# Attention with a seven-product query projection, exponentials summed by pairs of key blocks, and a new split of the PSUM banks

## Chip, cores and metric

The kernel runs on one core of one Trainium2 chip. The metric is the device time of one execution in microseconds (us). Several executions are timed and medians are quoted. All runs in this document were fast (granted TensorE clock 0.998 to 1.0 over the whole execution). Profiled figures come from one execution of each kernel.

Engines are named as the profile names them. PE is TensorE (matrix products), PEld is its weight loads, DVE is VectorE, ACT is ScalarE, and SP issues the DMA transfers. In these traces each of them takes its instructions in the order in which the program gives them. PSUM is the memory into which PE writes its products; it is used here in banks of 512 fp32 columns. An eviction is the copy of a bank out of PSUM by DVE.

## The reference

The reference is one transformer block with modulation. Only its first half, attention, is changed. Cut to that:

```python
# x: [1, 2048, 1024], k_cache and v_cache: [1, 32, 2048, 128], wq: [1024, 4096], wo: [4096, 1024], all bf16
h = _layernorm(x) * (1 + ca) + sa
q = (h @ wq).reshape(B, Sq, 32, 128).transpose(0, 2, 1, 3)
scores = jnp.einsum('bhqd,bhkd->bhqk', q, k_cache) * 128 ** -0.5
p = _softmax(scores, axis=-1)
o = jnp.einsum('bhqk,bhkd->bhqd', p, v_cache)
x = x + ga * (o.transpose(0, 2, 1, 3).reshape(B, Sq, 4096) @ wo)
# ... then a gated MLP with a spatial product, untouched by the change
```

## The kernel before

The unit to think in is a **half**: one head with 1024 of the 2048 queries, over 16 key blocks of 128 keys. There are 64 halves, indexed by `i`; `kb` is the key block in a half. For each key block PE computes a block of scores (keys on partitions, two matmuls of 512 queries), ACT takes the exponential of the 128x1024 block, and PE multiplies it with the values (two more matmuls). DVE adds the 16 blocks of exponentials into one block `pacc`, which gives the softmax denominators. Between these, PE does the query projection of a coming half: 16 matmuls, from the list `fill`, a few in each key block.

So a half has 32 score matmuls, 32 value matmuls and 16 projection matmuls, 80 in all, each 128x128 weights with 512 columns.

The query projection, eight matmuls (the 1024 channels in steps of 128) into one PSUM bank for 512 queries, and then one copy out by DVE:

```python
def side_ps(name, shape):
    return psum.tile(shape, FP32, name=name, tag="side", bufs=1)   # 1 PSUM bank
# bank_ps: 3 banks (value products and others); wide_ps: 2 tiles of 2 banks (scores)

def q_work(h, qh, new_ps=side_ps, outs=None):
    ...
        def one(n, j=j, box=box):
            ...
            nc.tensor.matmul(box["ps"][:], wq_t[:, dc, hc:hc + DH], src[:, dc, q0:q0 + 512],
                             start=(n == 0), stop=(n == KD - 1))
            if n == KD - 1 and outs is None:
                out(j, box)                        # DVE: copy the bank to qT
```

The loop over key blocks (cut):

```python
for g, (i, kb) in enumerate(steps):
    if kb == 0:
        o_ps = [bank_ps("ops", [P, 512]) for _ in range(2)]
    ...
    if i == len(halves) - 1:
        ...
        elif kb == 13:
            normalise(i - 1)                       # DVE: ou * rbc; rbc comes by DMA
    pt = att.tile([P, 1024], BF16, name="pt", tag="pt", bufs=5)
    nc.scalar.activation(pt[:], s_tiles.pop(g)[:], ACT.Exp, scale=SCALE)
    emit_s(g + 2)                                  # scores, two key blocks ahead
    ...
    for j in range(2):                             # value products of this key block
        nc.tensor.matmul(o_ps[j][:], vs[h][:, kb, :], pt[:, j * 512:(j + 1) * 512],
                         start=(kb == 0), stop=(kb == NKB - 1))
    if kb == 1:
        nc.vector.tensor_add(out=pacc[:], in0=pt_tiles[g - 1][:], in1=pt[:])
    elif kb > 1:
        nc.vector.tensor_add(out=pacc[:], in0=pacc[:], in1=pt[:])   # 15 dependent additions a half
    ...                                            # at kb 15 DVE copies o_ps to ou, one bank
    ...                                            # before this addition, one after it
    for fn in fill[:n]:                            # projection matmuls of a coming half
        fn()
```

The output projection and all later large products already use seven products of half size instead of eight (class `Block`). The query projection did not.

The softmax here doesn't subtract the row's maximum and nothing guards it: scores larger than these inputs give would overflow.

## Time and profile before

| | |
|---|---|
| median before | 1782.42 us (4 runs, 1782.16 to 1783.58) |
| profiled execution: span | 1780.5 us |
| start of the first exponential | 30.63 us |
| first exponential to the end of the last | 1119.92 us |
| from there to the end | 629.91 us |
| a half in the steady stretch | 17.29 us, for 80 matmuls |

The length of a half is read as the distance between the starts of DVE's first output copy (`ou<-ops`) in successive halves.

The head of the page of the kernel before gives the span, the busy time of each engine, and, in its part on the chain of work that ended last, the share of each engine in that chain:

```profile
span 1780.5 us, 25079 instructions
PE 1751.8 (98%) x8526; PEld 809.6 (45%) x8644; DVE 1490.5 (84%) x2567; ACT 1296.6 (73%) x1527; POOL 27.6 (2%) x39
...
PE 90%; DVE 6%; issue 2%; DMA 2%; ACT 0%; SPq 0%; POOL 0%; DVEq 0%; ACTq 0%; POOLq 0%
```

(`issue` is time in which an engine waited for nothing that the profile shows; names with a q are sequencers.) PE is both the busiest engine and 90% of the chain. The busy share alone would not settle it: 98% in this kernel. The Trainium skill, "Perfetto Trace Analysis", section "Identifying the Most-Contended Engine", calls matmul busy time no good measure of how close a kernel is to the roofline, because pipelined instructions look smaller in a trace. Here the chain and the timeline were read instead.

The timeline of PE in the steady stretch (start in us, duration, engine, source line, operation, output and inputs, partitions x elements, number of instructions in the row):

```profile
702.01 0.59 PE L379 MATMUL sps<-qT,kT 128*128 128x512 bf16 x2
702.44 0.59 PE L648 MATMUL ops<-pt,v_sb 128*128 128x512 bf16 x2
702.87 0.38 PE L358 MATMUL qps<-h1T,wq_t 128*128 128x512 bf16 x1
703.09 0.59 PE L379 MATMUL sps<-qT,kT 128*128 128x512 bf16 x2
```

Five matmuls start in 703.09 - 702.01 = 1.08 us, 0.216 us each, without a break (over long stretches 0.2159). The durations overlap, as the matmuls are pipelined, so it is the distance of starts that counts. 80 x 0.2159 = 17.27 us, within 0.02 us of a half. Here a matmul that is left out is worth 0.216 us, as long as nothing else sets the pace.

What the rest is shows in DVE's own timeline:

```profile
701.69 0.69 DVE L662 COPY ou<-ops 128x512 f32<-128x512 f32 x1
702.29 0.68 DVE L657 TENSOR_TENSOR pacc<-pt 128x1024 bf16<-128x1024 bf16 x1
...
708.21 3.87 DVE L659 TENSOR_TENSOR pacc<-pacc,pt 128x1024 bf16<-128x1024 bf16 x5
```

The copy and the addition after it have nothing to do with each other: they start 0.60 us apart although each lasts 0.68 to 0.69 (they overlap by 0.09). In the last row each addition needs the sum of the one before: five take 3.87 us, so they start (3.87 - 0.69) / 4 = 0.79 us apart.

Busy time in a window of 200 us of the steady stretch (columns as in the header), and all that PE waited for between the first and the last exponential (engine and line of the waiting instruction, what it waited for: us in total, number of waits, longest; waits of 0.15 us or less are not listed):

```profile
core 0: us, PE busy (x) PEld busy (x) DVE busy (x) ACT busy (x) POOL busy (x), PEclk, DMA share, GB/s
600.00:800.00 200.00, 199.05 (x909) 90.44 (x926) 175.40 (x279) 183.66 (x185) 0.00 (x0) 1.00 0.49 126
```

```profile
PE ops L648 <- DVE ou L655: 1.1, 3, 0.6
PE dps L482 <- DVE qT L348: 0.9, 2, 0.7
PE sps L379 <- ACT pt L636: 0.9, 2, 0.7
PE qps L358 <- DVE rec L486: 0.4, 1, 0.4
```

DVE is 175.40 / 200 = 87.7% busy and ACT 91.8%. PE waits 3.3 us in 1119.

### The profile page before, as it was taken

How to read it: one execution, taken by the hardware profiler on the slowest of the kernel's cores; microseconds unless marked ns; L12 is line 12 of the kernel's file. 1: busy time of each engine (PE TensorE's matmuls, PEld its weight loads, DVE VectorE, ACT ScalarE, POOL GpSimd, SP SyncE). 2: the span in 40 equal slices, each digit the busy share in tenths (PEclk: the TensorE clock that was granted, in tenths of full speed). 3: DMA queues.
4: the chain of work that ended last, by engine and by line, in shares of the span. 5: the costliest groups of instructions: out<-in, count | busy, mean ns of one | idle time of the engine just before them, and what ended most of it. 6: DMA issues, size and time to landing. Idle time of an engine off the chain costs nothing.

```text
span 1780.5 us, 25079 instructions
## 1 busy us (share of the span) xinstructions
PE 1751.8 (98%) x8526; PEld 809.6 (45%) x8644; DVE 1490.5 (84%) x2567; ACT 1296.6 (73%) x1527; POOL 27.6 (2%) x39
## 2 busy tenths in 40 slices
PE   7999999999999999999999999999999999999999
PEld 4444444444444444444444444444444444444444
DVE  6998888888888888888889888896679789775894
ACT  6898999999989999999999999811145666733610
POOL 1000000000000000000000000000000000000000
PEclk9999999999999999999999999999999999999999
DMA  8584656566455535455555633635658374564312
GB/s 248 128 178 99 148 149 142 136 155 158 109 140 151 137 96 151 118 135 159 132 160 138 153 102 95 175 106 174 162 153 226 90 172 123 177 148 136 89 48 71
DMA packets 445345, 247.84 MB, mean 139 GB/s; under 512 B 289312, under 2 KB 406560, under 8 KB 445216
## 3 DMA queue, kind: packets, MB, share of 16 engines
q1 hardware_dynamic: 445216, 246.23, 52.7%
q8 instruction: 67, 1.10, 0.3%
q14 instruction: 62, 0.51, 0.1%
HBM read 144.18 MB, written 52.71 MB: 111 GB/s over the span
## 4 chain that ended last, share of the span: by engine, by line
PE 90%; DVE 6%; issue 2%; DMA 2%; ACT 0%; SPq 0%; POOL 0%; DVEq 0%; ACTq 0%; POOLq 0%
PE ops L648 23%; PE sps L379 23%; PE a L762 15%; PE qps L358 12%; PE b L762 8%; PE c L762 4%; PE bo L1363 3%; DVE pacc L659 1%; DVE sum L810 1%; DMA wm<-in_w_mod_dram 1%; DMA oq<-oT_dram 1%; PE mps L185 0%; DVE stats L138 0%; PE a L1441 0%; DVE z_st L1098 0%
## 5 line engine op out<-in xcount | busy, mean ns | idle before, releaser
L636 ACT ACTIVATE pt<-sps 128x1024 bf16<-128x1024 f32 x1024 | 1018.7, 1024 | 105.2 <-PE sps L379 71.3
L659 DVE TENSOR_TENSOR pacc<-pacc,pt 128x1024 bf16<-128x1024 bf16 x882 | 605.5, 687 | 59.1 <-ACT pt L636 1.6
L648 PE MATMUL ops<-pt,v_sb 128*128 128x512 bf16 x1992 | 597.4, 379 | 6.6 <-DVE ou L655 1.1
L379 PE MATMUL sps<-qT,kT 128*128 128x512 bf16 x2000 | 598.5, 379 | 1.5 <-ACT pt L636 0.9
L358 PE MATMUL qps<-h1T,wq_t 128*128 128x512 bf16 x990 | 334.9, 379 | 1.4 <-DVE rec L486 0.4
L648 PEld LDWEIGHTS <-v_sb 128*128 128x128 bf16 x2048 | 200.1, 98 | 243.1 <-issue 1.5
L379 PEld LDWEIGHTS <-kT 128*128 128x128 bf16 x2048 | 198.9, 98 | 243.9 <-issue 6.6
L805 ACT ACTIVATE snap<-a 128x512 f32<-128x512 f32 (+1 forms) x114 | 62.7, 566 | 126.4 <-PE a L762 113.9
L358 PEld LDWEIGHTS <-wq_t 128*128 128x128 bf16 x992 | 97.0, 98 | 117.1
L1212 ACT ACTIVATE zr<-zr,z_nm,z_rs 128x256 f16<-128x256 f16 x166 | 83.0, 592 | 77.6 <-DMA zr<-z_dram 70.9
L348 DVE CAST qT<-qps 128x512 bf16<-128x512 f32 x124 | 85.7, 691 | 40.2 <-PE qps L358 39.3
L810 DVE TENSOR_TENSOR sum<-b,snap 128x512 f32<-128x512 f32 (+1 forms) x76 | 50.3, 662 | 48.6 <-PE b L762 28.7
L762 PEld LDWEIGHTS <-h_slots 128*128 128x128 f16 (+1 forms) x574 | 56.2, 98 | 66.2 <-issue 0.9
L495 DVE TENSOR_TENSOR oT<-ou,rbc 128x1024 bf16<-128x1024 f32 x62 | 75.6, 1219 | 2.3 <-DMA rbc<-rec_dram 2.0
L762 PEld LDWEIGHTS <-zr 128*128 128x128 f16 x456 | 44.6, 98 | 54.1 <-issue 0.4
L473 DVE TENSOR_REDUCE den<-pT 128x8 f32<-128x1024 bf16 x54 | 63.9, 1183 | 0.0
L762 PEld LDWEIGHTS <-oq 128*128 128x128 bf16 (+1 forms) x408 | 39.7, 98 | 49.3 <-DMA oq<-oT_dram 1.4
L655 DVE COPY ou<-ops 128x512 f32<-128x512 f32 x63 | 43.6, 691 | 21.2 <-PE ops L648 21.2
L1066 ACT ACTIVATE z<-sum 128x448 f16<-128x448 f32 x48 | 27.6, 575 | 26.0 <-DVE sum L810 25.7
L657 DVE TENSOR_TENSOR pacc<-pt 128x1024 bf16<-128x1024 bf16 x63 | 43.0, 683 | 2.4 <-ACT pt L636 2.4
L1363 PE MATMUL bo<-w_out,z1T 128*128 128x512 f16 x192 | 44.2, 379 | 0.0
L662 DVE COPY ou<-ops 128x512 f32<-128x512 f32 x63 | 43.2, 685 | 0.0
(305 smaller groups left out, 1609.0 us busy)
## 6 DMA issues: line engine op xcount, KB each, us to landing
rbc<-rec_dram SPq DMA_DIRECT2D x63, 512.0 KB
v_sb<-in_A_v_cache_dram SPq DMA_DIRECT2D x40, 512.0 KB
oT_dram<-oT SPq DMA_DIRECT2D x62, 256.0 KB
sums_dram<-pacc SPq DMA_DIRECT2D x54, 256.0 KB
wm<-in_w_mod_dram SPq DMA_DIRECT2D x12, 1024.0 KB
zr<-z_dram SPq DMA_DIRECT2D x23, 512.0 KB
wo<-in_A_wo_dram SPq DMA_DIRECT2D x16, 512.0 KB
oq<-oT_dram SPq DMA_DIRECT2D x15, 512.0 KB
```

The costliest lines, as they stand in the source:

```text
L348: nc.vector.tensor_copy(out=out_t[:, sl], in_=box["ps"][:])
L358: nc.tensor.matmul(box["ps"][:], wq_t[:, dc, hc:hc + DH], src[:, dc, q0:q0 + 512], start=(n == 0), stop=(n == KD - 1))
L379: nc.tensor.matmul(sps[:, j * 512:(j + 1) * 512], kts[h][:, kb * P:(kb + 1) * P], qts[(h, qh)][:, j * 512:(j + 1) * 512], start=True, stop ...
L473: nc.vector.tensor_reduce(out=den[:], in_=state[i]["pT"][:], op=ALU.add, axis=mybir.AxisListType.X)
L495: nc.vector.tensor_mul(out=oT, in0=state[i]["ou"][:], in1=state[i]["rbc"][:])
L636: nc.scalar.activation(pt[:], s_tiles.pop(g)[:], ACT.Exp, scale=SCALE)
L648: nc.tensor.matmul(o_ps[j][:], vs[h][:, kb, :], pt[:, j * 512:(j + 1) * 512], start=(kb == 0), stop=(kb == NKB - 1))
L659: nc.vector.tensor_add(out=pacc[:], in0=pacc[:], in1=pt[:])
L762: nc.tensor.matmul(self.ps[self.BANK[n]], a, b, start=(n in (1, 2, 7) and k == 0), stop=(k == len(lhs) - 1), skip_group_check=True)
L810: nc.vector.tensor_add(out=t, in0=ps, in1=snap)
L1212: nc.scalar.activation(z, z, ACT.Identity, scale=z_rs[:, q:q + 1], bias=z_nm[:, q:q + 1])
L1363: nc.tensor.matmul(bo, z1T[0, f // 2][:, f % 2, ti * P:(ti + 1) * P], wout[f // 2][:, f % 2, sl], start=(f == 0), stop=(f == NF - 1), skip ...
```

## The change

The intent is to take matmuls off PE, which paces attention, and to pay for them on DVE.

1. **Seven products instead of eight.** For the head pairs 5 to 14 (heads 10 to 29) the query projection of two heads and all 2048 queries is cut into 2 x 2 x 2 blocks and computed with seven half-size products on sums of blocks: 56 matmuls instead of 64 for a pair, 80 fewer in all. DVE makes the operand sums (fp16) and combines the products, with 14 evictions of PSUM banks for a pair instead of 8.
2. **Sums of exponentials by pairs of key blocks**: 7 additions of 2048 elements and one of 1024 for a half, instead of 15 of 1024.
3. **PSUM.** Three banks and one become two for value products and two (`qa`, `qb`) for the projection. The value products of key blocks 0 to 7 come one key block later, and two sets are issued at key block 8, so that DVE can empty both output banks before they are written again.
4. **Order.** A table `FILLS` says for each half how many projection matmuls go into each key block; tiles in SBUF are packed to make room; some weight loads move.

The diff, cut to its core:

```diff
-        return psum.tile(shape, dtype, name=name, tag="bank", bufs=3)
-    def side_ps(name, shape):
-        return psum.tile(shape, FP32, name=name, tag="side", bufs=1)
+        return psum.tile(shape, dtype, name=name, tag="bank", bufs=2)
+    def qa_ps(name, shape):
+        return psum.tile(shape, FP32, name=name, tag="qa", bufs=1)
+    def qb_ps(name, shape):
+        return psum.tile(shape, FP32, name=name, tag="qb", bufs=1)
...
+    def q_pair(n, j):
+        ...
+        def done(m):
+            a, b = box["a"][:], box["b"][:] if "b" in box else None
+            if m in (1, 6, 5):
+                nc.vector.tensor_copy(out=x if m == 6 else su, in_=a)
+            if m == 2:
+                out(h, 0, b, su)
+            elif m == 5:
+                out(h + 1, 1, b, su)
+            elif m == 3:
+                out(h + 1, 0, a, None)
+            elif m == 4:
+                out(h, 1, b, x)
+        def one(m, dc):
+            ...
+            nc.tensor.matmul(box["b" if m in (2, 7, 4) else "a"][:], *operand(m, dc),
+                             start=(m in (1, 2, 7) and dc == 0), stop=(dc == 3),
+                             skip_group_check=True)
+            if dc == 3:
+                done(m)
+        return [... for m in (1, 2, 6, 7, 5, 3, 4) for dc in range(4)]
...
-    FILL = [2, 1, 1, 1, 1, 1, 0, 1, 2, 1, 2, 2, 0, 0, 0, 1]
+    PAIRS = range(5, 15)
+    FILLS = {...
+             16: [3, 1, 1, 1, 1, 0, 1, 1, 0, 1, 1, 0, 1, 0, 1, 1],   # even halves 16..54
+             17: [3, 1, 1, 1, 0, 1, 1, 1, 0, 1, 1, 0, 1, 1, 0, 1],   # odd halves 17..55
+             56: [3, 1, 0, 1, 0, 1, 1, 0, 0, 1, 0, 1, 0, 1, 0, 0],
+             ...}
...
+        if 1 <= kb <= 8:
+            emit_pv(g - 1)
+        if kb >= 8:
+            emit_pv(g)
...
-        if kb == 1:
-            nc.vector.tensor_add(out=pacc[:], in0=pt_tiles[g - 1][:], in1=pt[:])
-        elif kb > 1:
-            nc.vector.tensor_add(out=pacc[:], in0=pacc[:], in1=pt[:])
+        if kb == 3:
+            sums2 = att.tile([P, 2, 1024], BF16, name="sums2", tag="sums2", bufs=1)
+            nc.vector.tensor_add(out=sums2[:], in0=pairs[g // 2 - 1][:], in1=pairs[g // 2][:])
+        elif kb % 2 and kb > 3:
+            nc.vector.tensor_add(out=sums2[:], in0=sums2[:], in1=pairs[g // 2][:])
         if kb == NKB - 1:
+            pacc = state[i]["pacc"] = ...
+            nc.vector.tensor_add(out=pacc[:], in0=sums2[:, 0], in1=sums2[:, 1])
```

The products 1, 6, 5 and 3 of a group accumulate in one bank, `qa`, one on top of the other, and DVE must copy out each partial sum before the next product goes on top of it.

## The prediction

> **What bounds the kernel now.** TensorE: the page gives PE 98% busy and 90% of the chain that ended last. Attention runs from the first exponential at 30.6 us to the last at 1149.5 us. The timeline at 700 us shows 512-column matmuls 0.216 us apart without a break; a half (16 key blocks of one head, 1024 queries) takes 17.28 us = 80 x 0.216: 32 scores, 32 value products, 16 query projections. My estimate for the part is 5100 x 0.216 = 1102 us plus about 14 us for small products, 1116 in all, so only about 4 us are lost, nearly all before 168 us. The waits view has PE waiting for DVE or ACT under 4 us in all. DVE is 86 to 90% busy here, ACT 91%; exponentials last 1024 ns but follow each other in 0.924 us where PE lets them (5 in 4.72 us), so ACT alone would need about 946 us.
>
> **What the change does.**
> 1. For heads 10 to 29 the query projection of two heads becomes seven half-sized products instead of eight: 56 matmuls instead of 64 per pair. The instruction order confirms 80 fewer. Worth 80 x 0.216 = 17.3 us, all on the critical engine.
> 2. DVE gains work: 14 evictions per pair instead of 8 (60 more, 0.69 us each), 40 weight differences of 512 elements (about 0.4 us, estimated), 16 activation sums of 1024 (0.69 us): 41 + 16 + 11 = 68 us.
> 3. To pay, exponentials are summed by pairs of key blocks: per half seven additions of 2048 (1.22 us, as the trace has for that shape) and one of 1024, 9.2 us, instead of fifteen of 0.687, 10.3 us: 70 us less. The Trainium skill, "VectorE: DVE Perf Modes", tier table, gives bf16 tensor_tensor 2x; 683 and 1218 ns for 1024 and 2048 elements agree: doubling saves only the fixed part. DVE's total stays, but a half shrinks to 78 matmuls, 16.85 us, so I expect DVE 90 to 93% busy.
> 4. PSUM goes from three banks plus one to two plus two. Value products start one step late in each half, so that DVE can empty both output banks: about 1.5 us of other matmuls cover two copies that start 0.61 us apart. The tight place in a seven-product group is from product 5 to 3 in one bank; the fill table leaves a step there.
> 5. Late loads and banks are rearranged; I expect 1 to 2 us either way.
>
> **Sum.** 17.3 us gained, less 3 to 4 us of new PE waits on DVE (evictions behind 1.22 us additions): about 1768 us. Range 1763 to 1778. Chances: faster by over 2% 0.02, within 2% 0.95, slower by over 2% 0.03.
>
> **What would show each step.** The last exponential starts near 1135 us; from 250 to 900 us a half takes about 16.9 us; 80 matmuls fewer at the same 0.216 us; 448 additions of 2048 elements at about 1.22 us; PE waits for DVE grow from about 3 to 5 to 8 us; ACT stays below 95% busy; from the last exponential to the end stays 631 us within 2 us.
>
> **What would make it wrong.** If DVE's in-order queue sets the pace (over 96% busy, PE waiting for query evictions in most groups), the gain shrinks to a few us or vanishes. If the packed early tiles wait for one another, the first exponential comes later than 30.6 us. If later output-weight loads or the slot order stall the output projection, the loss appears right after the last exponential. If the delayed value products remove stalls that I do not see, the gain exceeds 17 us.

## More of the kernel before

The costliest groups on the page (line, engine, operation, shapes, count | busy us, mean ns of one | idle time of the engine just before them, and what ended most of it):

```profile
L636 ACT ACTIVATE pt<-sps 128x1024 bf16<-128x1024 f32 x1024 | 1018.7, 1024 | 105.2 <-PE sps L379 71.3
L659 DVE TENSOR_TENSOR pacc<-pacc,pt 128x1024 bf16<-128x1024 bf16 x882 | 605.5, 687 | 59.1 <-ACT pt L636 1.6
...
L358 PE MATMUL qps<-h1T,wq_t 128*128 128x512 bf16 x990 | 334.9, 379 | 1.4 <-DVE rec L486 0.4
```

DVE's additions take 687 ns each, and DVE stood idle for 59.1 us just before them. A named wait accounts for only 1.6 us of the largest kind.

## The result

| | before | after |
|---|---|---|
| median, us | 1782.59 (12 runs, 1781.91 to 1783.88) | 1764.53 (8 runs, 1762.62 to 1765.49) |
| ratio after to before | | 0.9897, 95% interval 0.9887 to 0.9907 |
| profiled execution: span | 1780.5 | 1763.6 |
| start of the first exponential | 30.63 | 31.97 |
| first exponential to the end of the last | 1119.92 | 1098.36 |
| from there to the end | 629.91 | 633.30 |
| a half in the steady stretch | 17.29 (80 matmuls) | 16.84 (78 matmuls) |

A ratio is the mean time of one kernel's fast runs over the mean of the other's in the same rounds, so it is not quite the ratio of the medians. The medians differ by 18.1 us. The profiled executions differ by 16.8 us before rounding, in three terms that the table gives: +1.34, -21.56 and +3.39.

The page of the changed kernel, the lines that answer to those of before:

```profile
span 1763.6 us, 23669 instructions
PE 1732.4 (98%) x8447; PEld 800.2 (45%) x8564; DVE 1484.5 (84%) x2235; ACT 1306.1 (74%) x1527; POOL 29.7 (2%) x39
...
PE 90%; DVE 5%; DMA 2%; issue 1%; SPq 1%; ACT 1%; POOL 0%; DVEq 0%; ACTq 0%; POOLq 0%
```

The weight loads, of which none are missing here, fell from 8644 to 8564: the 80 matmuls. DVE's busy time is the same within 6 us. Its groups:

```profile
L804 ACT ACTIVATE pt<-sps 128x1024 bf16<-128x1024 f32 x1024 | 1028.3, 1024 | 76.9 <-PE sps L484 39.5
...
L824 DVE TENSOR_TENSOR sums<-sums,pt 128x2048 bf16<-128x2048 bf16 x384 | 466.6, 1215 | 16.5 <-ACT pt L804 9.0
...
L380 PE MATMUL qps<-h1T,wq_t 128*128 128x512 bf16 x342 | 115.2, 379 | 1.0 <-DVE rec L621 0.6
```

The idle time in front of the additions fell from 59.1 to 16.5 us, and 9.0 of the 16.5 are waits for an exponential. PE's timeline has the new fp16 products among the rest, at an unchanged distance of (704.13 - 703.05) / 5 = 0.216 us:

```profile
703.05 0.38 PE L465 MATMUL qa<-h1s,tx 128*128 128x512 f16 x1
703.26 0.59 PE L484 MATMUL sps<-qT,kT 128*128 128x512 bf16 x2
703.70 0.59 PE L742 MATMUL ops<-pt,v_sb 128*128 128x512 bf16 x2
704.13 0.38 PE L465 MATMUL qb<-h1s,tx 128*128 128x512 f16 x1
```

The busy time of two windows of the changed kernel, the same stretch as before and the last 111 us of attention (columns as in the header shown of before):

```profile
600.00:800.00 200.00, 199.05 (x911) 90.63 (x927) 182.57 (x234) 190.72 (x191) 0.00 (x0) 1.00 0.47 127
987.00:1098.00 111.00, 110.15 (x503) 49.88 (x511) 96.95 (x117) 108.28 (x112) 0.00 (x0) 1.00 0.58 150
```

DVE is 91.3% busy in the first, ACT 95.4%. In the second ACT is 108.28 / 111 = 97.5% busy. The three plain halves there with 71 matmuls (55, 56 and 62) take 15.59, 15.86 and 15.51 us where 71 x 0.2159 is 15.33: 0.26 + 0.53 + 0.18, about 1.0 us over. It looks as if the exponentials come near to setting the pace there; this is a reading of the trace, which no experiment tested.

All that PE waited for between the first and the last exponential of the changed kernel:

```profile
PE sps L484 <- ACT pt L804: 1.3, 3, 0.7
PE qps L380 <- DVE rec L621: 0.6, 1, 0.6
```

That is 1.9 us against 3.3. So there are fewer waits than before, not more.

**Where the 21.6 us of attention came from**, worked out from the two traces: 80 x 0.2159 = 17.3 us of matmuls; 2.9 us in halves 1 to 9, which took 4.6 us more than their matmul count before and 1.7 us after; about 1.4 us because the 50 or so steady halves shrank by 0.46 us and not by the 0.43 us of two matmuls; about 1 us in the last half, where before PE had waited for the last exponentials; less the 1.0 us of the late halves. The sum is 21.6.

**Where 3.4 us were given back.** After the last exponential PE's instructions are in the same order in both kernels. At the first block of the output projection the changed kernel is 20.0 us ahead. It then loses 1.2, 1.1, 0.6 and 0.3 us, and from there to the end it stays 16.8 us ahead. The waits at the two largest steps, and DVE's timeline a little earlier:

```profile
1135.74 3.61 PE L927 MATMUL a<-wo,h_slots 128*128 128x512 bf16 x16 [1.29 <-DVE wq_t L818]
...
1150.85 4.43 PE L927 MATMUL b<-wo_t,s_slots 128*128 128x512 f16 x16 [0.73 <-DVE wo_t L676]
```

```profile
1128.13 1.22 DVE L824 TENSOR_TENSOR sums<-sums,pt 128x2048 bf16<-128x2048 bf16 x1
1132.72 1.23 DVE L630 TENSOR_TENSOR s_slots<-ou,rbc 128x1024 bf16<-128x1024 f32 x1 [3.37 <-DMA rbc<-rec_dram]
1133.87 1.22 DVE L824 TENSOR_TENSOR sums<-sums,pt 128x2048 bf16<-128x2048 bf16 x1
1135.00 1.28 DVE L818 COPY wq_t<-ops 128x512 f32<-128x512 f32 x2
```

In brackets stands the idle time before a row and what ended it. (`wq_t` and `s_slots` are reused slots: L818 is the copy of the last value products out of PSUM, L630 is `normalise`.) In the last half DVE stood for 3.37 us in front of the normalisation of the half before, for the reciprocals that come by DMA, and everything behind it in DVE's queue, the copies that PE waits for among it, stood as well. In the kernel before that wait was 0.54 us:

```profile
1151.57 1.23 DVE L495 TENSOR_TENSOR oT_last<-ou,rbc 128x1024 bf16<-128x1024 f32 x1 [0.54 <-DMA rbc<-rec_dram]
```

The transfer itself is not slower. It was issued at 1147.0 us in the kernel before and at 1128.3 in the changed one, 4.6 and 4.4 us ahead of the normalisation. What differs is that DVE came to it 4.0 us after the issue before, and 1.05 us after it now.

**The 1.3 us at the start** are not the change. In twelve profiled executions of kernels that share the new first 30 us the first exponential starts between 30.31 and 31.97 us, and the profile of after has the latest of them. In the slice from 25 to 30 us the granted PE clock was 0.66 in that profile, and 1.00 in that of before. The Trainium skill, "TensorE: Matmul & The Clock Gate", section "What's actually happening", says that the clock is released after a busy window of about 3.4 us, that the window is free-running, and that the warm-up therefore differs from run to run. The scatter of 1.7 us fits that, and so does the clock that the traces record: of the twelve, only the three that start latest (after 31.97, e1 31.66, e9 31.20 us) have a stretch at half clock that lasts beyond 22 us. No experiment set the clock.

### The profile page after: what moved, and what is told of

It is laid out like the page before. It is cut to its first block, busy times and chain, and to the rows that moved or that the text cites. A ratio compares the mean times of both kernels' runs of the same rounds, so it can differ in the third digit from the quotient of the medians.

```text
span 1763.6 us, 23669 instructions
## 1 busy us (share of the span) xinstructions
PE 1732.4 (98%) x8447; PEld 800.2 (45%) x8564; DVE 1484.5 (84%) x2235; ACT 1306.1 (74%) x1527; POOL 29.7 (2%) x39
## 4 chain that ended last, share of the span: by engine, by line
PE 90%; DVE 5%; DMA 2%; issue 1%; SPq 1%; ACT 1%; POOL 0%; DVEq 0%; ACTq 0%; POOLq 0%
PE ops L742 24%; PE sps L484 24%; PE a L927 15%; PE b L927 8%; PE qps L380 4%; PE qa L465 4%; PE c L927 4%; PE qb L465 3%; PE bo L1530 3%; DVE sum L975 1%; DMA wm<-in_w_mod_dram 1%; DVE sums L824 1%; SPq L645 0%; PE mps L198 0%; DVE z_st L1264 0%
## 5 line engine op out<-in xcount | busy, mean ns | idle before, releaser
L804 ACT ACTIVATE pt<-sps 128x1024 bf16<-128x1024 f32 x1024 | 1028.3, 1024 | 76.9 <-PE sps L484 39.5
L824 DVE TENSOR_TENSOR sums<-sums,pt 128x2048 bf16<-128x2048 bf16 x384 | 466.6, 1215 | 16.5 <-ACT pt L804 9.0
L380 PE MATMUL qps<-h1T,wq_t 128*128 128x512 bf16 x342 | 115.2, 379 | 1.0 <-DVE rec L621 0.6
L818 DVE COPY ou<-ops 128x512 f32<-128x512 f32 x126 | 81.2, 686 | 35.6 <-PE ops L742 34.8
L1378 ACT ACTIVATE zr<-zr,z_nm,z_rs 128x256 f16<-128x256 f16 x82 | 41.2, 590 | 65.4 <-DMA zr<-z_dram 65.4
L822 DVE TENSOR_TENSOR sums<-pt 128x2048 bf16<-128x2048 bf16 x64 | 77.9, 1217 | 4.4 <-ACT pt L804 3.4
L630 DVE TENSOR_TENSOR oT<-ou,rbc 128x1024 bf16<-128x1024 f32 x62 | 75.6, 1219 | 2.7 <-DMA rbc<-rec_dram 2.7
L450 DVE COPY tx<-qa 128x512 f32<-128x512 f32 x60 | 41.3, 689 | 27.4 <-PE qa L465 27.4
L927 PEld LDWEIGHTS <-s_slots 128*128 128x128 f16 (+1 forms) x400 | 38.9, 98 | 49.8 <-issue 2.6
L465 PE MATMUL qa<-h1s,wq_t 128*128 128x512 f16 x160 | 57.4, 379 | 0.4
L380 PEld LDWEIGHTS <-wq_t 128*128 128x128 bf16 x352 | 34.4, 98 | 42.0 <-issue 0.7
L927 PEld LDWEIGHTS <-wq_t 128*128 128x128 f16 (+1 forms) x344 | 33.6, 98 | 38.7 <-DMA wq_t<-oT_dram 0.4
L465 PEld LDWEIGHTS <-wq_t 128*128 128x128 bf16 (+1 forms) x320 | 31.3, 98 | 37.8
```

The costliest lines, as they stand in the source:

```text
L380: nc.tensor.matmul(box["ps"][:], weights[:, dc, hc:hc + DH], src[:, dc, q0:q0 + 512], start=(n == 0), stop=(n == KD - 1))
L465: nc.tensor.matmul(box["b" if m in (2, 7, 4) else "a"][:], *operand(m, dc), start=(m in (1, 2, 7) and dc == 0), stop=(dc == 3), skip_group ...
L630: nc.vector.tensor_mul(out=oT, in0=state[i]["ou"][:], in1=state[i]["rbc"][:])
L804: nc.scalar.activation(pt_tiles[g], s_tiles.pop(g)[:], ACT.Exp, scale=SCALE)
L818: nc.vector.tensor_copy(out=ou[:, j * 512:(j + 1) * 512], in_=o_ps[j][:])
L822: nc.vector.tensor_add(out=sums2[:], in0=pairs[g // 2 - 1][:], in1=pairs[g // 2][:])
```

## Experiments

Each entry gives the edit, what was expected, what was measured, and what follows. Runs sent together shared a chip and the runs of the kernel before: e1 to e4 (before: 1782.44 us); e5, e7, e8 and e10 (1782.56); e9, e11 and e12 (1783.10); e13 (1782.23). All twelve results were correct against the reference.

The first question was whether the 18 us are the 80 matmuls, with the rest of the change as mere preparation, or whether the rest does something of its own.

### e1_eight: the whole change, but eight products

```diff
-    PAIRS = range(5, 15)
-    fill = [f for half in halves[1:20] for f in q_work(*half)]
-    fill += [(None, (n, j)) for n in PAIRS for j in range(2)]
+    PAIRS = range(0)
+    fill = [f for half in halves[1:] for f in q_work(*half)]
-             7: [...], 16: [...], 17: [...], 56: [...],      # FILLS: 16 matmuls a half (18 in the first)
-        if 8 <= i < 16 and kb in (6, 12):
-            h1_sum(1 + (i - 8) // 2, 2 * (i % 2) + kb // 12)
```

(The loads of the query weights went back to where eight products need them.)

> The changed kernel with the ordinary eight-product projection put back for all heads (and its fill table of 16 per half, its weight loads at the old halves, no operand sums); pair sums, late value products and banks stay as changed. Theory M (TensorE paces, time goes by the number of matmuls): 80 matmuls come back, 17.3 us slower than the changed kernel, about 1781.8 us; steady halves 17.29 us. Rival R (the gain comes from VectorE being relieved by the pair sums): within 5 us of the changed kernel, about 1765 to 1770 us.

Measured: 1778.95 us (1777.46 to 1780.99), ratio to before 0.9976 (0.9963 to 0.999). A steady half takes 17.27 us, attention 1114.97 us, the rest after it 632.59, so that most of what is lost after attention is lost with eight products too.

So the other parts of the change save 3.5 us without a matmul less. From here to the full change attention falls by 1114.97 - 1098.36 = 16.6 us (by the medians, from different rounds, 14.4). That is the 17.3 us less 0.7 to 3, of which the late halves account for 1.0. The measured 1778.95 lies between what the two theories said, nearer to M. With the rest of the change in place the matmuls are nearly the whole gain, but 3.5 us come from somewhere else.

### e2_single: the whole change, but single additions

```diff
-        if kb == 3:
-            sums2 = att.tile([P, 2, 1024], BF16, name="sums2", tag="sums2", bufs=1)
-            nc.vector.tensor_add(out=sums2[:], in0=pairs[g // 2 - 1][:], in1=pairs[g // 2][:])
-        elif kb % 2 and kb > 3:
-            nc.vector.tensor_add(out=sums2[:], in0=sums2[:], in1=pairs[g // 2][:])
-        if kb == NKB - 1:
+        if kb == 1:
             pacc = state[i]["pacc"] = ...
-            nc.vector.tensor_add(out=pacc[:], in0=sums2[:, 0], in1=sums2[:, 1])
+            nc.vector.tensor_add(out=pacc[:], in0=pt_tiles[g - 1], in1=pt_tiles[g])
+        elif kb > 1:
+            nc.vector.tensor_add(out=pacc[:], in0=pacc[:], in1=pt_tiles[g])
```

> The changed kernel with exponentials again added one key block at a time (15 additions of 1024 per half), all else as changed, seven products included. VectorE in a steady half was 91.3% busy in the changed kernel; my estimate is that it rises to about 95%. Theory M (TensorE paces and VectorE still has slack): within 2 us of the changed kernel, steady halves of 16.84 us, so the pair sums were not needed to pay. Rival R (without the pair sums VectorE becomes the pace): halves of over 17.1 us, 10 us or more slower than the changed kernel.

Measured: 1778.96 us (1776.29 to 1779.47), ratio 0.9976 (0.9964 to 0.9989). Halves 33 to 48 take 17.09 us on average, attention 1112.14.

The theory that the gain is in the matmuls, and that single additions would cost little, fell. Undoing one part of the change, with all 80 matmuls still saved, lost 14.4 of the 18 us (by medians of different rounds). The window of e2 and a row of DVE's timeline:

```profile
600.00:800.00 200.00, 198.20 (x900) 89.63 (x917) 188.76 (x311) 188.63 (x189) 0.00 (x0) 1.00 0.48 126
```

```profile
644.86 4.66 DVE L826 TENSOR_TENSOR pacc<-pacc,pt 128x1024 bf16<-128x1024 bf16 x6
```

DVE is only 94.4% busy, and yet in these 200 us the waits (above 0.15 us) list nothing at all that DVE waited for: it is never free. The 11 us in which it is not busy are gaps between additions that depend on one another: six in 4.66 us start (4.66 - 0.69) / 5 = 0.79 us apart, for a duration of 0.69. Counted in the trace of halves 33 to 48, 9 of the 15 additions of a half stand right in front of the one that needs their sum; in front of the other 6 DVE has something else to do. Of the 54.7 us that DVE was idle in front of these additions in the whole run, a named wait accounts for 0.8. This gave a new theory, D: an addition whose input is the sum just made starts 0.19 us later than one that is independent, about nine times a half; single additions fill DVE with that, and the pair sums pay for the change by making such steps fewer (3 a half), more than by their durations. Not all of the loss comes with the new work of DVE: of what e2's halves take longer than those of the change, 4.5 us fall in halves 1 to 9, where single additions cost 4.2 us with eight products too (e4 against e1, below), and about 10 us in the later ones.

### e3_pairs: the kernel before, with pair sums only

```diff
-        pt = att.tile([P, 1024], BF16, name="pt", tag="pt", bufs=5)
-        nc.scalar.activation(pt[:], s_tiles.pop(g)[:], ACT.Exp, scale=SCALE)
+        if kb % 2 == 0:
+            pair_prev = pair if kb else None
+            pair = att.tile([P, 2, 1024], BF16, name="pt", tag="pt", bufs=3)
+        pt = pair[:, kb % 2]
+        nc.scalar.activation(pt, s_tiles.pop(g)[:], ACT.Exp, scale=SCALE)
```

(and the additions as in the change; to make room in SBUF three tiles have one buffer less.)

> The kernel before with the pair sums alone (both output copies ahead of the additions at the end of a half; one buffer less for four small tiles to make room), old banks and value products at once. It asks where the 3.0 us gained in halves 1 to 9 beyond the matmul count come from. If from the pair sums (theory P): excess of halves 1 to 9 over the matmul count falls from 4.6 to about 1.7 us, total about 1779.5 us. If from the late value products (theory L): excess stays at 4 us or more, total 1782 us or more.

Measured: 1781.42 us (1779.86 to 1784.08), ratio 0.9994 (0.9982 to 1.0007). Not clearly different from before. Halves 1 to 9 lose 3.3 us over their matmul count, between what theory P (1.7) and theory L (4 or more) said. Where PE sets the pace and waits for little, relief for DVE is worth little.

### e4_late: eight products and single additions

The edit is e1 and e2 together: what is left of the change is the split of the PSUM banks, the late value products and the packing.

> The eight-product version of the changed kernel (first of this batch) with exponentials added one block at a time: late value products and two plus two banks without pair sums and without seven products. Theory L: excess of halves 1 to 9 over the matmul count is about 1.7 us as in the changed kernel. Theory P: it is 4 us or more as before. In both the output projection should keep the 3.2 us that it lost after the change, so the total is about 1782.5 us under L and 1785.5 us under P.

Measured: 1783.15 us (1782.39 to 1783.9), ratio 1.0004 (0.9991 to 1.0016); attention 1118.51 us. Not different from before. But a steady half takes 17.27 us here and in e1, 80 x 0.2159, and 17.29 to 17.30 in the kernel before and in e3: so the 0.03 us a half that the steady halves gained beyond their matmuls come with the late value products, the banks and the new order.

With e1, e2, e4 and the full change there are all four combinations of two choices, each with the late value products. The length of attention in the profile, and the median:

| | eight products | seven products | difference in attention |
|---|---|---|---|
| single additions | e4: 1118.51 us (1783.15) | e2: 1112.14 us (1778.96) | -6.4 us |
| pair sums | e1: 1114.97 us (1778.95) | after: 1098.36 us (1764.53) | -16.6 us |

The same 80 matmuls are worth 6.4 us with single additions and 16.6 us with pair sums. Neither the sums by pairs nor the new order alone does anything that can be seen in the median time (e3, e4), and together they give 3.5 us (e1). The traces place most of that in halves 1 to 9, where DVE also does the layer norm of the second half of the queries. Over their matmul count these halves lose 4.6 us before, 3.3 in e3, 5.6 in e4, 1.5 in e1 and 1.7 after. Why exactly they need both is not settled: e3 also had fewer buffers and another order of the two copies.

### e12_two: single additions in two chains

This is the test of theory D. It has as many additions of 1024 as e2 (14 here, and the closing one), the same durations, but even and odd key blocks go to two accumulators, so that no addition but the closing one needs the one just before it.

```diff
-        if kb == 3:
+        if kb == 2:
             sums2 = att.tile([P, 2, 1024], BF16, name="sums2", tag="sums2", bufs=1)
-            nc.vector.tensor_add(out=sums2[:], in0=pairs[g // 2 - 1][:], in1=pairs[g // 2][:])
-        elif kb % 2 and kb > 3:
-            nc.vector.tensor_add(out=sums2[:], in0=sums2[:], in1=pairs[g // 2][:])
+        if kb in (2, 3):
+            nc.vector.tensor_add(out=sums2[:, kb % 2], in0=pt_tiles[g - 2], in1=pt_tiles[g])
+        elif kb > 3:
+            nc.vector.tensor_add(out=sums2[:, kb % 2], in0=sums2[:, kb % 2], in1=pt_tiles[g])
```

> As the run with single additions (14.4 us slower than the changed kernel), but the 15 additions of 1024 per half go into two accumulators in turn, so that one addition does not read what the one just ahead of it wrote. In the single run, chains of five and six dependent additions took 3.87 and 4.66 us, 0.79 us from start to start for 0.69 us operations; independent neighbours elsewhere start 0.60 us apart. Theory D (VectorE was full there because of the gap behind each dependent addition, at only 94% busy): most of the loss goes, 1764 to 1769 us. Rival (the sum of the durations, 15 x 0.69 us, is what was too much): about as the single run, 1777 us or more.

Measured: 1765.1 us (1764.48 to 1766.76), ratio 0.9902 (0.9888 to 0.9916): the time of the full change. Halves take 16.84 us. The same window of e12, and a row of DVE's timeline:

```profile
600.00:800.00 200.00, 200.00 (x928) 90.73 (x927) 186.41 (x315) 190.62 (x191) 0.00 (x0) 1.00 0.48 127
```

```profile
623.91 3.09 DVE L825 TENSOR_TENSOR sums<-sums,pt 128x1024 bf16<-128x1024 bf16 x5
```

DVE is 93.2% busy, but now it waits for others again. The five additions start (3.09 - 0.68) / 4 = 0.60 us apart. By the medians (of different rounds) 13.9 of the 14.4 us that e2 had lost came back, with the same number of additions and the same work in them. (In the profiled attention it is 12.2 of 13.8; the rest lies in halves 1 to 9.) Theory D holds: what filled DVE in e2 was the gap in front of each addition that needs the one just before. The pair sums have it too (three additions of 2048 in 3.88 us start 1.33 us apart, independent operations of 1.22 us start 1.14 apart), but 3 times a half instead of 9. Taken from the traces of halves 33 to 48, from the start of each addition to the start of what DVE does next (waits above 0.15 us left out), the additions of a half take 10.7 us in e2 and in the kernel before, 9.0 by pairs and 9.2 in two chains.

### e8_dve1: one more operation of 1.2 us on DVE in each half

How near is the changed kernel to being paced by DVE? The normalisation is done twice in halves 16 to 55, with the same result.

```diff
-        nc.vector.tensor_mul(out=oT, in0=state[i]["ou"][:], in1=state[i]["rbc"][:])
+        for _ in range(2 if 16 <= i < 56 else 1):
+            nc.vector.tensor_mul(out=oT, in0=state[i]["ou"][:], in1=state[i]["rbc"][:])
```

> The changed kernel with one VectorE operation of 1.22 us per half done twice in halves 16 to 55 (the normalising product, same result). It asks how much room VectorE has. From 600 to 800 us VectorE sat waiting for TensorE or ScalarE for about 14 us in the changed kernel, 1.2 us per half of 16.84, so I expect the room to be just used up: 0 to 12 us slower (halves of 16.84 to 17.1). If the busy share of 91% tells the room (1.5 us per half), no change within 2 us. If VectorE already paced, 1.2 x 40 = 48 us slower.

Measured: 1767.03 us (1766.18 to 1769.56), ratio 0.9915 (0.99 to 0.993), 2.5 us over the 1764.53 of the change. The same window of e8:

```profile
600.00:800.00 200.00, 199.06 (x910) 90.58 (x927) 194.80 (x245) 190.58 (x191) 0.00 (x0) 1.00 0.46 127
```

40 times 1.2 us, 49 us of work, cost 2.5 us. DVE is 97.4% busy, more than the 94.4% of e2, and halves 33 to 48 take 16.85 us, so PE still keeps the pace. (Of the 3.1 us by which the halves of the profiled execution are longer, 1.6 fall in halves 49 to 56, where DVE also makes sums of the output weights, and 0.3 in halves 33 to 48.) My threshold of the prediction ("over 96% busy") was wrong in both directions. The Trainium skill, "Perfetto Trace Analysis", section "Identifying the Most-Contended Engine", calls the occupancy of VectorE a fair measure of how close one is to the roofline. It did not tell here whether the engine sets the pace: it did at 94.4% and did not yet at 97.4%, depending on how many operations needed the one just before. What told it was the time that the engine spends waiting for others. In the same 200 us it is 14.0 us in the changed kernel (the first three lines), 0.8 in e8 (the last) and none in e2:

```profile
DVE tx L450 <- PE qa L465: 9.2, 12, 1.0
DVE ou L818 <- PE ops L742: 3.4, 5, 0.9
DVE sums L824 <- ACT pt L804: 1.4, 8, 0.2
...
DVE ou L819 <- PE ops L743: 0.8, 3, 0.4
```

### e9_dve2: two more operations

The reduction of the denominators (1.18 us) is doubled as well.

```diff
-        nc.vector.tensor_reduce(out=den[:], in_=state[i]["pT"][:], op=ALU.add,
-                                axis=mybir.AxisListType.X)
+        for _ in range(2 if 16 <= i < 56 else 1):
+            nc.vector.tensor_reduce(out=den[:], in_=state[i]["pT"][:], op=ALU.add,
+                                    axis=mybir.AxisListType.X)
```

> The changed kernel with two VectorE operations per half done twice in halves 16 to 55 (the normalising product, 1.22 us, and the reduction of the denominators, 1.18 us; same results). With the first alone the room was just used up (2.5 us slower, VectorE waiting for others only 0.8 us in 200). If VectorE is full there, the second is paid in full: about 1.2 us in each of 40 halves, less some room in the eight halves with modulation products: 1800 to 1815 us, halves of about 18 us. If room were left, under 1775 us.

Measured: 1810.42 us (1808.95 to 1812.21), ratio 1.0156 (1.0142 to 1.017), 45.9 us over the change. The same window, and PE's longest waits in it:

```profile
600.00:800.00 200.00, 190.73 (x900) 85.36 (x899) 195.62 (x241) 178.30 (x179) 0.00 (x0) 1.00 0.44 116
```

```profile
PE qa L465 <- DVE tx L450: 5.0, 5, 1.0
PE ops L744 <- DVE ou L820: 3.7, 9, 1.1
```

The halves grew to 18.03 us. The first 1.2 us of extra work were nearly free (e8: 16.85 us for a half), and the next 1.18 us cost 1.18 us (18.03 - 16.85). The waits that the prediction had named are there now, and DVE waits for nothing in this window. So the changed kernel has about one operation's room on DVE for a half, and none beyond that.

### e10_nogap and e11_nogap2: the step that the fill table leaves

The prediction named product 5 and then product 3 in one bank as the tight place: DVE must copy out the bank in between. The first attempt was misplaced:

```diff
-             17: [3, 1, 1, 1, 0, 1, 1, 1, 0, 1, 1, 0, 1, 1, 0, 1],
+             17: [3, 1, 1, 2, 0, 0, 1, 1, 0, 1, 1, 0, 1, 1, 0, 1],
```

> The changed kernel with the fill table of odd halves changed so that the first matmul of product 3 directly follows the last of product 5, in the same bank, instead of two key blocks later. The copy that must come between takes 0.69 us on VectorE and can wait behind an addition of 1.22 us. If the tight place is real, TensorE loses about 0.9 us or more in each of 20 groups: 18 to 30 us slower than the changed kernel. If other slack hides it, within 3 us.

Measured: 1764.71 us (1764.32 to 1765.44), ratio 0.99 (0.9885 to 0.9915), no change. The trace shows why it says nothing: the moved matmul was the first of product 1, behind product 4 in the other bank. The second attempt:

```diff
-             16: [3, 1, 1, 1, 1, 0, 1, 1, 0, 1, 1, 0, 1, 0, 1, 1],
+             16: [3, 1, 1, 1, 1, 0, 1, 1, 0, 1, 1, 0, 2, 0, 0, 1],
```

> The test of the tight place once more, at the right place: the earlier run moved the first matmul of product 1 behind product 4, which is another bank and costs nothing. Here, in even halves, the first matmul of product 3 directly follows the last of product 5 in the same bank (by the instruction order), instead of two key blocks later. The copy of the bank on VectorE lies between them, 0.69 us plus what it waits for. If the tight place is real, TensorE loses about 0.9 us or more in each of 20 groups: 15 to 30 us slower than the changed kernel. If not, within 3 us.

Measured: 1782.92 us (1782.0 to 1783.75), ratio 1.0001 (0.9988 to 1.0013). PE's timeline at the place, and what PE waited for there from 300 to 1010 us:

```profile
654.04 0.38 PE L465 MATMUL qa<-h1s,wq_t 128*128 128x512 f16 x1
655.20 0.38 PE L465 MATMUL qa<-h1s,wq_t 128*128 128x512 f16 x1 [0.78 <-DVE tx L450]
```

```profile
PE qa L465 <- DVE tx L450: 15.6, 20, 0.8
```

The two matmuls start 1.16 us apart instead of 0.216. One matmul moved in a table, and each of 20 even halves loses 0.94 us (17.78 instead of 16.84), 18.4 us by the medians against the change: the whole gain. No work was added. This part of the prediction was right: without the two key blocks that the table puts between products 5 and 3, nothing is left of the gain.

### e7_both: an eleventh pair

Heads 8 and 9 also get seven products (8 matmuls fewer, taken from halves 12 to 15), and the bank rotation of e5 below is included.

```diff
-    PAIRS = range(5, 15)
-    fill = [f for half in halves[1:20] for f in q_work(*half)]
+    PAIRS = range(4, 15)
+    fill = [f for half in halves[1:16] for f in q_work(*half)]
+             12: [3, 1, 1, 2, 1, 2, 1, 2, 0, 1, 1, 1, 1, 1, 1, 1],   # 20; so have 13, 14, 15
...
-        if 8 <= i < 16 and kb in (6, 12):
-            h1_sum(1 + (i - 8) // 2, 2 * (i % 2) + kb // 12)
+        if 8 <= i < 12 and kb in (3, 6, 9, 12):
+            h1_sum(i - 7, kb // 3 - 1)
```

> The changed kernel with heads 8 and 9 made a seven-product pair too (11 pairs, operand sums made in halves 8 to 11, fills of halves 12 to 15 cut from 22 to 20), and the bank shift of the run before. If TensorE paces these halves, 8 matmuls fewer are worth 8 x 0.216 = 1.7 us, with the shift 2.9 us in all: about 1761.6 us. If the extra VectorE work at halves 11 to 15 paces instead, 1763 us or more.

Measured: 1762.91 us (1762.44 to 1763.44), ratio 0.989 (0.9874 to 0.9907). Halves 12 to 15 take 18.13 us instead of 18.56, 4 x 0.43 = 1.7 us. Against e5 on the same chip the medians differ by 1.3 us. These halves behave as the count of matmuls says; the shift of the banks gave nothing (e5), so the time missed the 1761.6 us expected.

### e5_tail: the banks of the first blocks after attention

This was the first theory of the 3.4 us given back: the rotation of banks makes the second block of the output projection wait for a bank that DVE empties late.

```diff
-    Block.count = 0
+    Block.count = 1
...
-    finish_here(2 * H - 1)
+    finish_here(2 * H - 1, bank_ps)
```

> The changed kernel with only the bank rotation at the start of the output projection shifted by one, so that its first new block takes the bank that is free (and the last denominators take one of the two output banks). The changed kernel waited there 1.3 us for the copies of the last attention outputs. Theory: the wait is the price of two banks plus two, and the shift takes it away: 1.2 us faster than the changed kernel, about 1763.3 us, and no wait of a matmul for the output copies after the last exponential. Rival: the wait moves to the next block that needs the other bank, and the total stays.

Measured: 1764.24 us (1763.51 to 1765.08), ratio 0.9897 (0.9882 to 0.9912), no change. The wait of 1.29 us is gone, and another one stands a little later in PE's timeline:

```profile
1142.07 1.90 PE L927 MATMUL a<-h_slots,os 128*128 128x512 f16 x8 [0.94 <-DVE os L997]
```

The bank was not the cause. DVE was late with everything, and whichever of its products PE needed first got the wait. That pointed to what held DVE up.

### e13_norm: the normalisation behind the copies

The kernel is e7, and in the last half the normalisation that waits for a DMA goes behind the two copies of the value products instead of in front of them.

```diff
-            elif kb == 13:
-                normalise(i - 1)
...
                 nc.vector.tensor_copy(out=ou[:, j * 512:(j + 1) * 512], in_=o_ps[j][:])
+            if final:
+                normalise(i - 1)
             fills(i, kb)
```

> The version with 11 pairs and the bank shift (1762.9 us), with one more edit: in the last half the normalising product of the half before it is issued after the two output copies instead of at key block 13. In the changed kernel VectorE, which works in order, stood 3.4 us at that product for the landing of the reciprocals (0.5 us in the kernel before), with the last pair sum, the output copies and the operand sums of the output projection behind it. Theory: this head-of-line wait is the cause of what the output projection lost after the change (about 3 us from the last exponential on; the bank wait was only where it showed first). Then the waits of 0.9 us for operand sums and 0.7 us for weight sums go, and the part from the last exponential to the end falls from 633.6 to 632 us or less: about 1761 us. Rival: VectorE simply has too much to do there, and the waits come back later: 1762.5 us or more.

Measured: 1760.07 us (1759.82 to 1761.37), ratio 0.9878 (0.9861 to 0.9894). The time from the last exponential to the end is 630.83 us, where e7 has 633.6. DVE's timeline in the last half of e13:

```profile
1127.65 1.29 DVE L820 COPY wq_t<-ops 128x512 f32<-128x512 f32 x2
1129.32 1.23 DVE L634 TENSOR_TENSOR s_slots<-ou,rbc 128x1024 bf16<-128x1024 f32 x1 [0.38 <-DMA rbc<-rec_dram]
```

The wait for the DMA is 0.38 us instead of 3.37 (3.17 in e7), because DVE does the copies while the transfer is under way, and PE's waits for `os` and `wo_t` are gone. So 2.7 us of the loss after attention came back, and their cause is shown: one instruction at the head of DVE's queue waited for a transfer, and what PE needed stood behind it. The last 0.9 us over the 629.91 of the kernel before are not explained. (e7 and e13 ran on different chips; the kernel before differed by 0.3 us between them, and no run of e13 is as slow as the fastest of e7.) This version beats both kernels: 22.2 us under the kernel before by the medians.

## Why the prediction was right or wrong

**The time.** 1768 us were predicted (1763 to 1778) and 1764.5 measured: in the range and in the predicted class, within 2%, but 3.5 us lower. The mechanism was right, and three terms of the sum had the wrong size.

- **"17.3 us gained" from 80 matmuls: right.** The weight loads fell by exactly 80, the distance of matmuls stayed at 0.216 us, halves went to 16.84 us where 16.85 was predicted. e1 against the full change gives 16.6 us in attention.
- **"less 3 to 4 us of new PE waits on DVE": wrong, and this is the step that failed.** PE's waits in attention fell from 3.3 to 1.9 us instead of growing to 5 to 8. I thought that the doubled additions would be in the way of the evictions. In fact they relieved DVE: I had reckoned them by durations (10.3 to 9.2 us for a half) and not seen the 0.19 us in front of each dependent addition, although it was in the page, as 59.1 us of idle time with hardly a cause named. By starts it is 10.7 to 9.0 us, a relief of 1.7 us instead of 1.1. That covers the new evictions and weight differences of the prediction (41 + 16 us in 40 halves, 1.4 us each); the 1.1 us would not have. Without the relief the waits would have been far worse than I said: e2 loses 14 us.
- **Not foreseen: about 3 us in halves 1 to 9, and 1.4 us in the steady halves.** The prediction said of the late value products that they might "remove stalls that I do not see". Stalls were removed: the 1.4 us come with the late products, the banks and the new order (e4). For the early halves e3 and e4 show that neither the late products nor the pair sums do it alone. It takes both (e1). The last exponential started at 1129.3 us and not near 1135.
- **"from the last exponential to the end stays 631 us within 2 us": missed.** The 631 counted from the start of the last exponential; so counted it was 634.3 in the profile, 3.4 us more than before. The prediction named later weight loads and slots as the risk. The cause of 2.7 us of it was the order of DVE's queue in front of a DMA (e13).
- **The tight place "from product 5 to 3 in one bank; the fill table leaves a step there": right.** Filling the step costs 0.94 us each time (e11).
- **"DVE 90 to 93% busy": right** (91.3% in the window). **"ACT stays below 95%": wrong**, 95.4% in that window and 97.5% at the end of attention, where it cost about 1.0 us as the trace is read.
- **"DVE's in-order queue sets the pace (over 96% busy ...)": the danger was real, the threshold was not.** It sets the pace at 94.4% in e2 and does not at 97.4% in e8.
- **"448 additions of 2048 elements at about 1.22 us": right**, 384 of 1215 ns in the group shown and 64 more of 1217 ns. The Trainium skill, "VectorE: DVE Perf Modes", section "The perf-mode tier table", gives 1224 ns for 2048 elements of bf16, which agrees.
- **The first exponential later by 1.3 us** in the profile of after is scatter of the start and not a wait of packed tiles: other runs with the same start are at 30.3 us.
- **How near the time came is in part luck.** In the profiled executions the gains that were not foreseen (2.9 + 1.4 + 1.0 us) and the losses that were not (1.3 at the start, 1.0 in the late halves, 3.4 after attention) nearly cancel.

**What stays open.** Why the early halves need both the pair sums and the late value products; what the exponentials cost in the last halves, which was read and not tested; and the 0.9 us after attention that e13 leaves.

## What to carry to other kernels

When work is put on an engine that is not the bottleneck, cost it by the distances of starts and not by durations: idle time in front of a group that no wait explains can be, as here, the gap between dependent operations, and two accumulators in turn removed it. Whether the engine had room was told here by how long it waits for others, not by its busy share; doubling one of its operations measures it. And in an in-order queue, look at what stands behind an instruction that waits for a DMA, above all at the end of a stage, where the next stage needs it at once.

## What the Trainium skill lacked or had wrong

- "VectorE: DVE Perf Modes", section "The DRAIN you can't avoid", says that the next operation waits for the pipe to empty unless it is free to start earlier, that a semaphore between operations costs nothing extra (eight copies, measured), and that reading straight away what the operation just before wrote is not safe without one; the page's "Rules for kernel authors" advise counting operations and not semaphores. The page gives no time for an operation that needs the result of the one just before. Here independent neighbours of 0.68 to 0.69 us start 0.60 us apart (e12), dependent additions 0.79 us (before, e2); for 1.22 us operations it is 1.14 and 1.33. These 0.19 us decided 14 us of the time, at an equal number of additions.
- "Perfetto Trace Analysis", section "Identifying the Most-Contended Engine", calls VectorE's occupancy a fair measure of how close one is to the roofline. As a measure of whether VectorE sets the pace it failed here: it did at 94.4% (e2) and did not yet at 97.4% (e8, whose room was nearly used up). The section does not propose the time that the engine waits for others as a measure of room, which did tell them apart (none and 0.8 us in 200 us, against 14.0 in the changed kernel).
- "TensorE: Matmul & The Clock Gate", section "Back-to-back issue gap", gives about 131 ns for each matmul of 512 columns in a sustained stream of weight loads and matmuls, and 216 ns for the isolated gap. Here the sustained distance was 215.9 ns over some 1100 us at a granted clock of 1.0, with a weight load for every matmul. The measurement agrees with the figure for the isolated case and not with the other. The page's own section "Wait — 56ns, not 53.3ns?" has a measured distance for back-to-back matmuls that agrees with this case too, so the two sections differ.
